# First keys and queries as float32 through SyncE and ScalarE, and units 2 to 7 in another order

## The chip, the cores and the metric

The kernel runs on one core of one Trainium2 chip. A core has five engines with instruction streams of their own: TensorE (PE in the profile; its weight loads are listed as PEld), VectorE (DVE), ScalarE (ACT), GpSimd (POOL) and SyncE (SP). Data moves between the main memory and the on-chip memory by DMA; an engine issues a DMA, and 16 DMA engines carry it out. The metric is the device time of one execution in microseconds; lower is better. Tests of the kernel before gave 285.56, 285.60 and 286.12 us, median 285.6.

## The reference

A sliding-window attention is followed by a two-layer network with a quick GELU. All inputs and the output are float32.

```python
B, H, S, D = 8, 8, 576, 64            # q, k, v: each 9.4 MB
scores = q @ k.T / sqrt(D)            # per batch and head
scores = where(|i - j| <= 32, scores, -1e9)
attn = softmax(scores)
x = (attn @ v) as [B * S, H * D]      # 4608 rows of 512
h = x @ w_in                          # w_in: 512 x 2048
out = (h * sigmoid(1.702 * h)) @ w_out   # w_out: 2048 x 512
```

## The kernel before

The 4608 rows are cut into 36 units of 128 queries (shifted by 32 rows against the keys, so that a window of 32 on both sides needs one unit of keys and 64 more) and into 9 tiles of 512 rows, four units each. For a unit, `scores` multiplies keys by queries and takes the exponential on ScalarE, `band` multiplies by a 0/1 mask on VectorE, `values` multiplies by v, with a column of ones that gives the sum, and `norm` divides on VectorE. `odd_v` copies v into a second arrangement, shifted by 64 rows, that every second block of queries needs: part 0 from the unit's own v, part 1 from the next unit's. `x_T` (one unit) and `x_T2` (two) transpose the result on TensorE for layer 1.

For a tile, layer 1 is either plain (`layer1_plain`: one step `d` of 256 columns of w_in, for one half of the tile's rows, eight matmuls and one GELU) or by seven products instead of eight (`l1_group`), which needs sums of weights (`w1_sums`, `w2_sums`) and of data (`x_sums`, `g_sums`) from VectorE. Tile 0 is computed plainly, tiles 1 to 8 by seven products. Layer 2 of a tile runs mixed into the next tile's layer 1: `self.do(self.l2, n)` takes the next n of its matmuls off a list.

The order of all this is written out by hand: each engine executes its instructions in the order of the program, and the framework adds only the waits for data and buffers. PSUM has banks with the tags A, B, C, E, LA, LB and t (two banks); a step that takes a tag waits until the one that had it before is read.

`opening` (L561) does the first units and tile 0. Its inputs come through POOL's DMA queue, which casts float32 to 16 bits on the way, in this order: first keys (320 rows) and first queries (256 rows) of batch 0, v of units 0 to 2, the first quarter of w_in, the second keys and second queries (256 rows each, up to the end of unit 3), the second quarter of w_in, v of units 3 and 4, the third quarter, keys and queries of units 4 to 7 (`load_four`), the fourth quarter, v of units 5 and 6, the first quarter of w_out, v of units 7 and 8, the rest of w_out, and then loads unit by unit (`fetch`). Between these issues POOL also builds the identity (`make_identity`) and the mask (`setup_mask`, `cut_mask`). A POOL issue waits, by the trace, until the load that stands eight places before it has landed.

`T_first` (L156) transposes the first or second keys or queries on TensorE; each half of the heads goes to one bank, and VectorE or ScalarE copies it out. Where TensorE has to wait at the start, `keep_busy` gives it junk matmuls on a zeroed tile. `first_layer1` (L845) is layer 1 of tile 1; its list `dv` holds VectorE's sums, taken off between the products.

## Time and profile before

| what | value |
| --- | --- |
| median of three runs | 285.6 us |
| the profiled execution's own time | 285.75 us |
| its span, first to last instruction | 284.0 us |
| granted TensorE clock | 1.000 |
| PE busy | 272.8 us, 96% |
| DVE busy | 217.2 us, 76% |
| ACT busy | 193.9 us, 68% |
| POOL busy | 126.9 us, 45% |
| PE busy from 0 to 24 us / 24 to 45 us / 45 to 284 us | 17.45 / 20.52 / 234.78 us |
| read from main memory / written to it | 36.83 MB / 9.44 MB |

A line of the timeline gives start, duration, engine, source line, operation, the tile written and the tile read, shapes, and in brackets how long the engine stood idle before it and what ended that. A line of the table of stages gives for a stretch of time its length, then the busy time (and number of instructions) of PE, PEld, DVE, ACT and POOL, the granted clock, the share of the DMA engines and the GB/s that they wrote. A line of the chain gives start, duration and whose work the end waited for. Times are from the start of the span. PE's time from 0 to 24 us holds junk as well as work, and its matmuls overlap, so that a busy PE need not be one at its peak.

### The profile page before, as it was taken

The page shows a single profiled execution, that of the slowest core. Times are in us where ns is not written, and L with a number is a line of the kernel's source. Part 1 is how long each engine was busy: PE and PEld are TensorE (multiplying, and loading weights), DVE is VectorE, ACT ScalarE, POOL GpSimd, SP SyncE. Part 2 cuts the span into 40 slices and gives each one's busy share as a digit, 9 for nine tenths or more (in the row PEclk, how much of TensorE's full clock was granted, in tenths as well). Part 3 has the DMA queues.
Part 4 walks back from the last instruction along what each step waited for, and adds up shares of the span by engine and source line. Part 5 has one row for each costly group of instructions (what it writes and reads, how often), then busy time and mean ns, then how long its engine had stood idle before and what let it go on. Part 6 is the DMA issues. An engine that isn't in the chain of part 4 may idle for free.

```text
span 284.0 us, 8953 instructions
## 1 busy us (share of the span) xinstructions
PE 272.8 (96%) x3684; PEld 223.3 (79%) x3684; DVE 217.2 (76%) x501; ACT 193.9 (68%) x340; POOL 126.9 (45%) x192
## 2 busy tenths in 40 slices
PE   6787999999999998999999999999999999999995
PEld 2466847776778887888888888888888888888884
DVE  1754997898887877798879887878788878946731
ACT  2556684799886778667966796689658875568411
POOL 8975446898599726739083909340110000000000
PEclk9999999999999999999999999999999999999999
DMA  8999999999999999999999999995422030201024
GB/s 90 182 193 196 184 204 159 193 124 147 136 154 152 200 127 195 124 203 143 201 102 189 131 203 82 198 146 140 132 58 71 26 113 14 81 2 74 2 95 133
DMA packets 149610, 37.63 MB, mean 132 GB/s; under 512 B 138048, under 2 KB 145216, under 8 KB 149568
## 3 DMA queue, kind: packets, MB, share of 16 engines
q0 software_dynamic: 106000, 18.42, 95.0%
q1 hardware_dynamic: 43120, 18.10, 34.2%
q8 instruction: 29, 0.48, 0.7%
q10 hardware_dynamic: 448, 0.52, 0.6%
q14 instruction: 13, 0.11, 0.1%
HBM read 36.83 MB, written 9.44 MB: 163 GB/s over the span
## 4 chain that ended last, share of the span: by engine, by line
PE 82%; DMA 7%; DVE 5%; POOL 4%; issue 1%; ACT 0%; DVEq 0%; POOLq 0%
PE o L70 37%; PE h L70 36%; PE pv L70 4%; DMA w<-in_moe_w_in_dram 4%; DMA xT<-x 3%; PE sc L70 3%; POOL ve L198 1%; POOL kq L142 1%; DVE xs L353 1%; DVE vo L209 1%; PE tp L321 1%; PE tp L231 1%; DVE a L334 1%; PE tp L188 1%; POOL w L115 1%
## 5 line engine op out<-in xcount | busy, mean ns | idle before, releaser
L418 ACT ACTIVATE g<-h 128x512 f16<-128x512 f32 x128 | 72.2, 598 | 35.7 <-PE h L70 34.9
L70 PEld LDWEIGHTS <-g 128*128 128x128 f16 x576 | 54.4, 98 | 9.5
L70 PEld LDWEIGHTS <-a 128*128 128x128 f16 x512 | 49.1, 97 | 12.3 <-DVE xs L353 2.2
L70 PE MATMUL h<-xs,a 128*128 128x256 f16 x384 | 57.6, 272 | 0.9 <-DVE xs L353 0.7
L70 PE MATMUL o<-w,g 128*128 128x256 f16 (+1 forms) x320 | 55.5, 294 | 0.0
L70 PEld LDWEIGHTS <-w 128*128 128x128 f16 x512 | 48.9, 98 | 8.4 <-DMA w<-in_moe_w_in_dram 1.7
L70 PE MATMUL h<-xT,w 128*128 128x256 f16 x384 | 54.0, 273 | 1.4 <-DMA w<-in_moe_w_in_dram 1.4
L209 POOL COPY vo<-ve 64x264 int32<-64x264 int32 x55 | 25.5, 463 | 61.3 <-PE pv L70 59.0
L70 PEld LDWEIGHTS <-gs 128*128 128x128 f16 x384 | 36.8, 98 | 4.7
L255 ACT ACTIVATE p<-sc 128x512 bf16<-128x512 f32 x72 | 36.9, 620 | 2.6 <-PE sc L70 2.5
L70 PE MATMUL o<-b,gs 128*128 128x256 f16 x256 | 37.6, 273 | 0.0
L70 PE MATMUL o<-b,g 128*128 128x256 f16 x256 | 37.5, 273 | 0.0
L198 POOL DMA_DIRECT2D ve<-in_v_dram x40 | 34.4, 865 | 6.2 <-DMA qst<-in_q_dram 2.8
L431 DVE TENSOR_TENSOR h<-h,s 128x512 f32<-128x512 f32 x32 | 22.3, 698 | 17.8 <-PE h L70 17.5
L131 POOL DMA_DIRECT2D qst<-in_q_dram x35 | 28.1, 804 | 3.5 <-DMA w<-in_moe_w_out_dram 2.8
L67 ACT COPY h<-h 128x512 f32<-128x512 f32 x32 | 18.9, 589 | 15.5 <-PE h L70 15.1
L293 DVE TENSOR_TENSOR x<-pv,rec 128x256 f16<-128x256 f32 (+1 forms) x53 | 27.6, 520 | 1.8
L131 POOL DMA_DIRECT2D kst<-in_k_dram x31 | 26.4, 855 | 5.0 <-DMA ve<-in_v_dram 2.6
L437 DVE TENSOR_TENSOR h<-h,s 128x512 f32<-128x512 f32 x32 | 22.4, 700 | 4.6 <-PE h L70 3.9
L263 DVE TENSOR_TENSOR p<-p,mask 128x1024 bf16<-128x1024 bf16 x36 | 25.0, 698 | 0.8 <-ACT p L255 0.6
L67 ACT COPY s<-h 128x512 f32<-128x512 f32 x32 | 19.2, 599 | 2.0 <-PE h L70 0.7
L70 PE MATMUL h<-xs,w 128*128 128x256 f16 x128 | 19.2, 273 | 0.0
(83 smaller groups left out, 343.7 us busy)
## 6 DMA issues: line engine op xcount, KB each, us to landing
out_dram<-o_sb SPq DMA_DIRECT2D x33, 256.0 KB, 4.6
ve<-in_v_dram POOLq DMA_DIRECT2D x32, 128.0 KB, 6.6
kst<-in_k_dram POOLq DMA_DIRECT2D x25, 128.0 KB, 6.6
qst<-in_q_dram POOLq DMA_DIRECT2D x21, 128.0 KB, 6.1
w<-in_moe_w_in_dram POOLq DMA_DIRECT2D x4, 512.0 KB, 8.9
w<-in_moe_w_out_dram POOLq DMA_DIRECT2D x4, 512.0 KB, 12.6
qst<-in_q_dram POOLq DMA_DIRECT2D x7, 96.0 KB, 6.4
kq<-in_q_dram POOLq DMA_DIRECT2D x2, 256.0 KB, 5.9
```

What stands on the lines that cost most here:

```text
L67: (eng.copy if eng is self.nc.scalar else eng.tensor_copy)(out, in_)
L70: self.nc.tensor.matmul(out, lhsT, rhs, start=start, stop=stop, skip_group_check=True)
L115: self.nc.gpsimd.dma_start(self.w1[:, :, c * 512:c * 512 + w], self.w_in[:, c * 512:c * 512 + w].rearrange("(k p) f -> p k f", p=128))
L131: self.nc.gpsimd.dma_start(t[off:off + n], src[b, :, s:s + n, :].rearrange("h s d -> s h d"))
L198: self.nc.gpsimd.dma_start(t[off:off + n, :, :self.D], self.v[b, :, s:s + n, :].rearrange("h s d -> s h d"))
L209: eng.tensor_copy(*((words(vo[64:128]), words(self.ve[u % 9][64:128])), (words(vo[0:64]), words(nxt)))[i])
L255: self.nc.scalar.activation(p[:, eo].rearrange("k h s -> k (h s)"), sc[eo], AF.Exp, scale=self.scale)
L263: (eng or self.nc.vector).tensor_mul(pv, pv, msk.to_broadcast([128, 8, 2, SQ]))
L293: dve.tensor_mul(x[:, 4 * at:4 * (at + n), :].rearrange("p (b h) d -> p b h d", b=n), acc[:, :, :, :D], r.to_broadcast([128, n, 4, D]))
L418: act.activation(g[:, f, 256 * half:256 * half + 256], bank.rearrange("p (i n) -> p i n", i=2), AF.Gelu_apprx_sigmoid)
L431: dve.tensor_add(e, b, s7)
L437: dve.tensor_add(c, b, s7)
```

## The change

The first keys and first queries no longer go through POOL with a cast. SP and ACT load them as float32, SP heads 0 to 3 into partitions 0 to 63 and ACT heads 4 to 7 into partitions 64 to 127, two DMAs each. New functions `cast` and `early` turn them into bfloat16 in the tile that also takes the second keys and queries: of the keys VectorE casts three of five row groups and ScalarE two, of the queries each two of four. The first queries lie four rows to a partition instead of two. `T_first` transposes them from both halves of the partitions in turn, and can leave one copy for later (`late_copy`).

The identity and the mask come from one `iota` on POOL and small VectorE operations, and the mask is cut by VectorE. `load_w1` takes a column instead of a quarter's number.

In the opening, there are fewer junk matmuls; the second keys are transposed between x_T of units 0 and 1, the second queries before layer 1's first step; the scores of units 2 and 3 stand before its second step; units 2 and 3 are transposed one by one, one copy on VectorE and one on ScalarE. The second quarter of w_out is loaded before v of units 7 and 8. The odd_v copies of units 6 and 7 move from ahead of the first band to between the norms; one step of layer 1 moves between values(6) and values(7); and w1_sums((3,), 1) moves from the opening to the head of `dv` in `first_layer1`. Later on, x_T2(10) becomes x_T of units 10 and 11.

```diff
@@ -97,23 +97,27 @@
         self.spark = cst.tile([128, 1], F32, name="spark")
     def setup_mask(self):
...
+        D = self.work.tile([128, 128], F32, name="gap", tag="s7", bufs=2)
+        self.nc.gpsimd.iota(D, pattern=[[-1, 128]], base=0, channel_multiplier=1,
+                            allow_small_or_imprecise_dtypes=True)
+        dve = self.nc.vector
+        dve.tensor_single_scalar(self.ident, D, 0.0, op=ALU.is_equal)
+        dve.tensor_copy(self.identh, self.ident)
+        for r in (slice(0, 64), slice(64, 128)):
+            d = D[r, r].rearrange("p (b s) -> p b s", b=1).to_broadcast([64, 2, SQ])
+            up = int(r.start > 0)
+            for blk, op in ((2 * up, ALU.is_ge), (2 - 2 * up, ALU.is_le)):
+                dve.tensor_single_scalar(self.mask[r, blk:blk + 2, :], d, 0.0, op=op)
     def cut_mask(self):
         lo, hi = slice(0, 64), slice(64, 128)
         for b, rows, cols in ((0, hi, slice(0, 32)), (0, lo, slice(32, 64)), (2, lo, slice(0, 32)), (2, hi, slice(32, 64))):
-            self.nc.gpsimd.memset(self.mask[rows, b, cols], 0.0)
-    def load_w1(self, c, n=1):
-        w = 512 * n
-        self.nc.gpsimd.dma_start(self.w1[:, :, c * 512:c * 512 + w],
-                                 self.w_in[:, c * 512:c * 512 + w].rearrange("(k p) f -> p k f", p=128))
+            self.nc.vector.memset(self.mask[rows, b, cols], 0.0)
+    def load_w1(self, lo, n=512):
+        self.nc.gpsimd.dma_start(self.w1[:, :, lo:lo + n],
+                                 self.w_in[:, lo:lo + n].rearrange("(k p) f -> p k f", p=128))
     def load_w2(self, c):
         self.nc.gpsimd.dma_start(self.w2[:, 4 * c:4 * c + 4, :],
@@ -132,15 +136,34 @@
-    FIRST = {"k": ((0, 320, 5, 0), (320, 256, 2, 5)), "q": ((32, 256, 2, 7), (288, 256, 2, 9))}
+    FIRST = {"k": ((0, 320, 5, 0), (320, 256, 2, 5)), "q": ((32, 256, 4, 0), (288, 256, 2, 7))}
     def load_first(self, c, part):
-        if "first" not in self.stage:
-            self.stage["first"] = self.sb("g", [128, self.H, 11, self.D], BF16, 2, "kq1")
         lo, n, j, at = self.FIRST[c][part]
-        src = {"q": self.q, "k": self.k}[c]
-        self.nc.gpsimd.dma_start(self.stage["first"][0:n // j, :, at:at + j],
-                                 src[0, :, lo:lo + n, :].rearrange("h (p j) d -> p h j d", j=j))
+        src = {"q": self.q, "k": self.k}[c][0, :, lo:lo + n, :].rearrange("h (p j) d -> p h j d", j=j)
+        if part:
+            if "first" not in self.stage:
+                self.stage["first"] = self.sb("g", [128, self.H, 9, self.D], BF16, 2, "kq1")
+            self.nc.gpsimd.dma_start(self.stage["first"][0:n // j, :, at:at + j], src)
+            return
+        s = self.stage["early", c] = self.sb(*{"k": ("g", [128, 4, j, self.D], F32, 2),
+                                               "q": ("xs", [128, 4, j, self.D], F32, 1)}[c], "early")
+        for i in range(2):
+            (self.nc.sync, self.nc.scalar)[i].dma_start(s[64 * i:64 * i + 64], src[:, 4 * i:4 * i + 4])
+    def cast(self, c, engs):
+        at = 0
+        for eng, m in engs:
+            self.copy(eng, self.early(c)[:, :, at:at + m], self.stage["early", c][:, :, at:at + m])
+            at += m
+    def early(self, c):
+        j = self.FIRST[c][0][2]
+        h = 4 * (c == "q")
+        return self.stage["first"][:, h:h + 4, 0:j]
     def kq_tile(self, t):
@@ -158,16 +181,27 @@
         lo, n, j, at = self.FIRST[c][part]
         lo -= 32 * (c == "q")
         dst = self.kq_tile(0)["kq".index(c)][:, :, lo:lo + n]
-        r = slice(0, n // j)
-        src = self.stage["first"][r]
-        for i, (tag, eng) in enumerate(zip(tags, engs)):
-            tp = self.bank(tag, [128, 2, j, n // j], BF16, "tp")
-            for h in range(4):
-                for x in range(j):
-                    self.nc.tensor.transpose(tp[64 * (h % 2):64 * (h % 2) + 64, h // 2, x, :],
-                                             src[:, 4 * i + h, at + x, :], self.ident[r, r])
-            self.copy(eng, dst[:, 2 * i:2 * i + 2, :].rearrange("x h (p j) -> x h p j", j=j),
-                      tp.rearrange("x h j p -> x h p j"))
+        m = n // j
+        tps = [self.bank(tag, [128, 2, j, m], BF16, "tp") for tag in tags]
+        def one(i, h, x):
+            if part:
+                r, src = slice(0, m), self.stage["first"][0:m, 4 * i + h, at + x, :]
+            else:
+                r = slice(64 * i, 64 * i + 64)
+                src = self.early(c)[r, h, x, :]
+            self.nc.tensor.transpose(tps[i][64 * (h % 2):64 * (h % 2) + 64, h // 2, x, :], src, self.ident[r, r])
+        both = [(i, h, x) for i in range(2) for h in range(4) for x in range(j)]
+        for y in both if part else sorted(both, key=lambda y: y[::-1]):
+            one(*y)
+        for i, eng in enumerate(engs):
+            ap = (dst[:, 2 * i:2 * i + 2, :].rearrange("x h (p j) -> x h p j", j=j),
+                  tps[i].rearrange("x h j p -> x h p j"))
+            if eng is None:
+                self.late_copy = lambda e, ap=ap: self.copy(e, *ap)
+            else:
+                self.copy(eng, *ap)
     def load_four(self, c):
@@ -568,35 +602,36 @@
             dve.memset(t[:, :, self.D:], 1.0)
         self.load_first("k", 0)
         self.load_first("q", 0)
-        make_identity(nc, self.ident)
+        self.setup_mask()
+        self.cut_mask()
         act.activation(self.spark, self.spark, AF.Exp)
...
         self.load_w1(0)
-        self.setup_mask()
         self.load_first("k", 1)
         self.load_first("q", 1)
-        self.cut_mask()
-        self.load_w1(1)
+        self.load_w1(512)
         self.load_v(3)
         self.load_v(4, slice(0, 1))
-        self.load_w1(2)
+        self.load_w1(1024)
         self.load_v(4, slice(1, 2))
         self.load_four("k")
         self.load_four("q")
-        self.load_w1(3)
-        dve.tensor_copy(self.identh, self.ident)
-        self.keep_busy(10, "E", 512)
+        self.load_w1(1536)
+        self.keep_busy(8, "E", 512)
+        self.cast("k", ((dve, 3), (act, 2)))
+        self.cast("q", ((dve, 2), (act, 2)))
         self.T_first("k", 0, "AC", (dve, act))
-        self.keep_busy(2, "E", 512)
+        self.keep_busy(1, "E", 512)
         self.T_first("q", 0, ("LA", "LB"), (dve, act))
...
         self.load_w2(0)
+        self.load_w2(1)
         for u in (7, 8):
             self.load_v(u)
-        for c in (1, 2, 3):
+        for c in (2, 3):
             self.load_w2(c)
         self.load_kq("k", 8)
         self.scores(0, "t")
@@ -610,11 +645,12 @@
         self.norm(0)
         self.values(1, "AC")
         self.norm(1)
-        self.keep_busy(2, "E", 512)
-        self.x_T(0, "LA", act)
         self.keep_busy(1, "E", 512)
-        self.x_T(1, "LB", act)
-        self.T_first("k", 1, "AC", (dve, dve))
+        self.x_T(0, "t", act)
+        self.T_first("k", 1, ("LA", "LB"), (None, dve))
+        self.x_T(1, "B", act)
+        self.late_copy(act)
+        self.T_first("q", 1, "EC", (dve, act))
         h, n, gelus = [], [0], []
         def l1(half, *ds):
@@ -622,26 +658,26 @@
                 self.layer1_plain(0, d, half, h[n[0] % len(h)])
                 n[0] += 1
-        self.layer1_plain(0, 0, 0, "B", gelus)
-        self.T_first("q", 1, ("LA", "LB"), (dve, act))
-        self.layer1_plain(0, 1, 0, "E", gelus)
-        self.odd_v(2, dve)
-        self.odd_v(3, dve, (0,))
-        h[:] = ["B", "E", "LA", "LB"]
+        self.layer1_plain(0, 0, 0, "A", gelus)
         self.scores(2, "t")
-        self.scores(3, "AC")
+        self.scores(3, "BE")
+        self.layer1_plain(0, 1, 0, "C", gelus)
+        self.odd_v(2, dve, (0,))
+        self.band(2)
+        self.odd_v(2, dve, (1,))
+        self.odd_v(3, dve)
         self.layer1_plain(0, 2, 0, "LA", gelus)
+        self.values(2, "t")
+        self.band(3)
+        self.norm(2)
         self.layer1_plain(0, 3, 0, "LB", gelus)
+        self.values(3, "BE")
         self.do(gelus)
-        self.band(2)
-        self.odd_v(3, dve, (1,))
-        self.band(3)
-        self.values(2, "t")
-        self.norm(2)
-        self.values(3, "AC")
         self.norm(3)
+        h[:] = ["A", "C", "LA", "LB", "B", "E"]
         l1(0, 4)
-        self.x_T2(2, "A", dve)
+        self.x_T(2, "t", dve)
+        self.x_T(3, "B", act)
         l1(0, 5)
         dve.tensor_copy(self.k_first, self.kT[0][:, :, 0:64])
         dve.tensor_copy(self.v_first, self.ve[0][0:64])
@@ -653,6 +689,7 @@
         dve.tensor_copy(self.kT[4][:, :, 0:64], halo)
         l1(1, 2, 3)
         self.T_four("q", "AC", (dve, act))
+        h[:], n[0] = ["LA", "LB"], 0
         l1(1, 4, 5)
         self.odd_v(4, dve)
         self.scores(4, "t")
@@ -660,8 +697,7 @@
         self.odd_v(5, dve)
         for i in (3, 1, 2, 4):
             self.w1_sums((i,), 0)
-        self.odd_v(6, dve)
-        self.odd_v(7, dve, (0,))
+        self.odd_v(6, dve, (0,))
         for d, tag in ((6, "B"), (7, "E")):
             self.layer1_plain(0, d, 0, tag, gelus)
         self.do(self.l2, 3)
@@ -672,27 +708,27 @@
         self.do(self.l2, 2)
         self.band(4)
         self.band(5)
-        self.odd_v(7, dve, (1,))
         self.band(6)
         self.values(4, "t")
         self.norm(4)
+        self.odd_v(6, dve, (1,))
         self.band(7)
+        self.odd_v(7, dve, (0,))
         self.values(5, "AC")
         self.norm(5)
+        self.odd_v(7, dve, (1,))
         self.do(self.l2, 8)
         self.values(6, "t")
         self.norm(6)
-        self.do(self.l2, 2)
+        h[:], n[0] = "BE", 0
+        l1(1, 6)
         self.values(7, "AC")
         self.norm(7)
-        h[:] = "BE"
-        n[0] = 0
-        self.w1_sums((3,), 1)
-        l1(1, 6, 7)
+        l1(1, 7)
         self.x_T2(4, "A", act)
         self.do(self.l2, 2)
         self.x_T2(6, "t", dve)
-        self.do(self.l2, 4)
+        self.do(self.l2, 6)
     def fetch(self, u):
         self.load_kq("q", u)
@@ -826,7 +862,8 @@
         self.norm(11)
         self.scores(14, "BE")
         do(more, 8)
-        self.x_T2(10, "C", dve)
+        self.x_T(10, "A", dve)
+        self.x_T(11, "C", act)
         self.scores(15, "t")
         do(self.x_sums(2))
         self.seed2 = dve
@@ -844,7 +881,7 @@
     def first_layer1(self):
-        dv = [lambda i=i: self.w1_sums((i,), 1) for i in (1, 2, 4)]
+        dv = [lambda i=i: self.w1_sums((i,), 1) for i in (3, 1, 2, 4)]
         for n in range(4):
             if n == 3:
                 self.turn(12)
```

7 lines of the change are left out of this document (removed).

## The prediction

> **What bounds the kernel now.** I read the page's slices first: TensorE (PE) is full from the third slice to the last, so the end moves only by what the opening gains or what PE work grows. Here is PE and what the DMA engines wrote:
>
> ```profile
> PE   6787999999999998999999999999999999999995
> GB/s 90 182 193 196 184 204 159 193 124 147 136 154 152 200 127 195 124 203 143 201 102 189 131 203 82 198 146 140 132 58 71 26 113 14 81 2 74 2 95 133
> ```
>
> Then a table of stages. Up to 24 us PE is busy 17.45 us, some of it junk matmuls; in 24 to 45 us it lacks 0.48 us:
>
> ```profile
> 0.00:24.00 24.00, 17.45 (x314) 10.64 (x314) 12.93 (x41) 12.00 (x20) 18.50 (x35) 1.00 1.42 159
> 24.00:45.00 21.00, 20.52 (x346) 15.11 (x344) 16.84 (x36) 14.03 (x22) 10.34 (x13) 1.00 1.55 192
> ```
>
> In single microseconds the last column (GB/s written) climbs slowly, then stays between 154 and 217 with no gap; the loads shrink float32 to 16 bits, so twice that is read. Around 38 us PE (third number) is short:
>
> ```profile
> 2.00:3.00 1.00, 1.00 (x4) 0.35 (x3) 0.00 (x0) 0.30 (x2) 1.00 (x2) 1.00 0.21 9
> 3.00:4.00 1.00, 1.00 (x4) 0.41 (x3) 0.20 (x1) 0.00 (x0) 0.93 (x4) 1.00 0.76 68
> 4.00:5.00 1.00, 1.00 (x5) 0.21 (x2) 0.00 (x0) 0.00 (x0) 1.00 (x2) 1.00 1.32 191
> 7.00:8.00 1.00, 0.99 (x18) 0.48 (x16) 0.53 (x2) 0.61 (x1) 0.88 (x3) 1.00 2.42 154
> 16.00:17.00 1.00, 1.00 (x22) 0.69 (x20) 0.74 (x2) 0.01 (x1) 0.75 (x2) 1.00 1.24 208
> 38.00:39.00 1.00, 0.70 (x15) 0.19 (x8) 0.97 (x3) 1.00 (x3) 0.62 (x1) 1.00 1.24 198
> 39.00:40.00 1.00, 0.84 (x33) 0.69 (x34) 1.00 (x3) 0.98 (x2) 0.12 (x1) 1.00 1.24 207
> ```
>
> The chain of the opening runs over POOL's issues, then one load (w1 columns 1024 to 1535), then PE:
>
> ```profile
> 13.27 10.13 DMA w<-in_moe_w_in_dram
> 23.40 0.05 issue
> 23.44 1.05 PE h L70 x8
> ```
>
> The timeline shows every earlier step starting as its load lands: transposes of the second keys at 14.75, of the second queries at 16.30, layer 1 on w1's second quarter at 18.75. So the opening follows the DMA stream, and that stream is full from 4 us on. What matters is when it starts. From 35.6 us it is so again with w2: layer 2's first matmuls (35.75) and its next eight (39.90) start as POOL is let go by a landed w2 quarter (35.66, 39.88).
>
> **The change, part by part.** *First keys and queries.* POOL loses two issues (0.82 and 0.90 us); SP and ACT each get two. POOL starts the first one at 1.33, and bytes come slowly: 77 KB by 4.0 us, which at 191 GB/s is 0.4 us of full flow, so the stream is as if it had begun at 3.6. SP and ACT are free at 0.82 (ACT's first instruction; SP's wait is the same 0.8). What SP needs from issue to flow is shown by the last stores:
>
> ```profile
> 275.09 5.63 SPq L459 DMA_DIRECT2D out_dram<-o_sb  x3
> ```
>
> and by the bytes written in each quarter of a microsecond behind that issue:
>
> ```profile
> 275.50:275.75 0.25, 0.25 (x5) 0.23 (x3) 0.00 (x0) 0.14 (x1) 0.00 (x0) 1.00 0.00 0
> 275.75:276.00 0.25, 0.25 (x5) 0.23 (x3) 0.00 (x0) 0.24 (x1) 0.00 (x0) 1.00 0.20 70
> 276.00:276.25 0.25, 0.25 (x5) 0.22 (x4) 0.00 (x0) 0.00 (x0) 0.00 (x0) 1.00 1.04 352
> ```
>
> Issue at 275.09, as if begun at 275.95: 0.86 us. So the new stream begins at 0.82 + 0.86 = 1.7, 1.9 earlier. If the slow climb (first bytes about 2.75, full from 3.6: 0.85) belongs to the first reads and not to POOL, it begins at 0.82 + 0.66 + 0.85 = 2.35, 1.25 earlier. A store isn't a load; I take 1.6 and keep 1.25 and 1.9. The bytes read are the same. That they are also written as float32 costs nothing if reading limits; see the rival below.
>
> *The path of units 0 and 1.* k reads 0.655 MB, q 0.524 MB; at 2 x 191 GB/s that is 1.7 and 1.4 us. From 2.0 on, with the 0.7 us that lay between k's bytes (3.6 + 1.7 = 5.3) and its transposes (6.01), k lands at 4.4 and q at 5.8, up to 6.5 where v's packets mix in; I take 6.1. The casts are new. ACT's 512 elements: 0.58 (its 128x512 copies). DVE's 768 and 512: no row; 0.69 for 128x512 float32 from PSUM above, 0.217 for a 128x256 bf16 copy (so 0.43) below; I take 0.58. q: 6.1 + 0.58, 32 transposes at 0.87/40 us each (0.7), copy 0.69: scores at 8.1 against 8.64. At the bad end (q 6.5, cast 0.69, transposes 0.7 beneath k's copy of 0.82 on DVE, then q's 0.69: 8.7) they start when they do now, or 0.5 later if DVE's casts take twice that. Behind DVE's wait for q are the copies of transposed k and so both units' scores. Units 0 and 1 then end x_T(1)'s transposes near 14.2 now and 13.7 after; the second queries land 16.3 - 1.6 = 14.7. So even a start 0.5 later is covered, and this path costs and gives nothing.
>
> *Mask, identity, cut.* POOL loses some 2.8 us (0.22 + 0.29 + 0.36 + 4 x 0.29 + 4 x 0.14) and gets one iota, about 0.29 like the 128x128 select. DVE gets six small operations of 0.2 (the 128x128 cast is 0.195) and four memsets of about 0.1, 1.6 us, between iota's end near 1.9 and k's landing at 4.4; 0.5 or so would spill into the casts if each took twice that. POOL then reaches the second keys' issue near 5.0 instead of 8.67: 3.6 earlier, more than the stream's 1.6, so issuing doesn't hold it. Later issues wait for the load eight before, as now (w1's last waits 1.56 for its second), and so move with the stream.
>
> Does DVE's work hold POOL's issues? Three v issues take 2.66 us with DVE's 0.195 us cast among them, 0.89 each, the median of all: not visible. I take nothing; the other end is a rival below.
>
> *Units 2 and 3.* The order changes (k1 before x_T(1), scores before the second layer-1 step, split x_T with half the copies on ACT), with about the same operations. From the second queries to scores is 1.55 us (16.30 to 17.85), to the last norm's end 7.3 (23.63). From 14.7 that ends at 22.0, beside w1's third quarter at 21.8. No gain or loss besides the stream's; x_T's copy on ACT, 0.58, waits behind four gelus but lies beside a layer-1 step of 0.9.
>
> *Junk* falls from 20 to 15 matmuls, all beneath waits. The first ones take 0.42 us each until 4.24, then 0.22; eight last till 4.65, still past that point. If not, transposes run at half speed for about 1 us, in the covered path.
>
> *Units 4 to 7.* odd_v of units 6 and 7 (1.28 us plus a 0.35 us wait for v7) leaves its place before the first band; w2's second quarter goes ahead of v7 and v8, arriving 0.52 MB or 1.3 us earlier. Now PE lacks 0.30 + 0.16 in 38 to 40 us, waiting for bands. That goes: at most -0.5, since PE lacks 0.48 in all there. Against it w1_sums(3, 1), 0.68, moves into first_layer1, where DVE is busy 9.2 of 10 us (50 to 60): up to +0.7. v7 then comes 2.6 us later relative to the stream (1.05 MB), 36.5 - 1.6 + 2.6 = 37.5, and its copy now stands after norm(4), near 38: not late. I take -0.4. The late x_T2(10) becomes two transposes and copies: 0 (bounds +-0.2, one more instruction in a full PE).
>
> **Sum.** -1.6 - 0.4 = -2.0 on the profiled execution's own 285.75 (span 284.0 and 1.75 around it): 283.75. It stands 0.15 over the median of 285.6, so 283.6. Its own range, from 285.6: 1.9 + 0.5 + 0.2 off gives 283.0; 1.25 off and 0.2 on, with nothing from units 4 to 7, gives 284.55.
>
> **Rivals.** *Only issue time is saved.* The Trainium skill (DMA: Bandwidth & Descriptors, Issuing engines are not separate DMA queues) says DMAs of all issuers share the same engines, and more issuers save only the time to initiate. As a mechanism here: flow is limited after the issue, and the start moves only 1.33 - 0.82 = 0.5. For it: the slow climb may be the reads'. Against: 1.42 us from POOL's issue to bytes, 0.66 from SP's. Time: 285.6 - 0.5 - 0.4 = 284.7. Chance 0.11.
>
> *The DVE bill.* DVE holds POOL for as long as its new work lasts, 1.6 us of mask and some 0.9 us of casts beside POOL's issues; POOL's lead over the stream is 3.6 - 1.6 = 2.0, so 0.5 comes through, and w1_sums adds its 0.7: 285.6 - 1.6 - 0.4 + 1.2 = 284.8; chance 0.08. Against the first half stands the 0.89 us above, against the second nothing but the 0.8 us that DVE has free in 50 to 60. The Trainium skill (SBUF — State Buffer, SBUF: two separate sides) has the first half as a rule: a float32 copy from SBUF to SBUF on DVE locks GpSimd out, which then can't write descriptors. The trace of before has no such copy, so it neither shows nor denies it.
>
> *Slower: writing float32 limits.* No load of now writes over 217 GB/s. If that is a limit of loads, k and q (1.18 MB) take 5.7 us at 207 instead of 3.1, the whole stream is 2.6 - 1.6 = 1.0 later, and the time is 285.6 + 1.0 - 0.4 = 286.2. It decides from 1.18 MB / (3.1 + 2.0) us = 231 GB/s downward. Against it: float32 stores run at 352 above. Chance 0.09.
>
> **Chances and range.** The forecast 0.68; better than its range (PE also fills part of its idle before 24 us) 0.04; the rivals 0.28 as given. Measurement tells apart about 0.2%, 0.57 us: faster is under 285.03. Faster: forecast, better and 0.09 of the two middle rivals' 0.19, 0.81. Within 0.2%: 0.07 of those two, where the gain of units 4 to 7 fails too. Slower: the float32 rival and their last 0.03, 0.12. Range 282.6 to 285.6, leaving out the slower cases and a little below.
>
> **What would show it.** Right: GB/s over 150 by 2 to 3 us, near 380 written while k and q arrive; transposes at about 5; second queries' transposes near 14.7; layer 1 on w1's third quarter at 21.8 instead of 23.44; PE full in 38 to 40; everything after the same with an offset of 2. Wrong: written rate near 200 in the first microseconds; the casts starting after 6; POOL's issues stretched over 1 us while DVE casts; scores of unit 2 later than 17; PE gaps for DVE sums in 47 to 62.

## The result and the profile after

The changed kernel is slower: 287.26 us, median of five runs (286.62 to 287.86), against 285.60 for before on the same chip (five runs, 285.35 to 286.12). The ratio is 1.0054, with a 95% interval of 1.0032 to 1.0076. The forecast was 283.6, with a range up to 285.6. The profiled execution took 287.26 us, its span 285.5, so it is 1.5 us longer than the one of before both ways.

The page's slices of the changed kernel show where it went. A digit is the busy share of a slice of 7.1 us in tenths, for PEclk the granted clock. TensorE is at 50% in the first two slices, where it had 60 and 70%, and its granted clock falls in the second:

```profile
PE   5599999999999998999999999999999999999995
...
PEclk9689999999999999999999999999999999999999
...
GB/s 151 179 193 195 194 194 163 195 136 147 138 136 137 190 131 200 152 178 137 202 118 184 129 183 122 210 119 149 125 58 69 33 110 15 79 2 76 1 106 119
```

The table of stages of the changed kernel (length, then busy time of PE, PEld, DVE, ACT and POOL, granted clock, DMA share, GB/s written):

```profile
2.00:3.00 1.00, 1.00 (x4) 0.43 (x3) 0.88 (x6) 0.85 (x1) 1.00 (x2) 1.00 0.54 114
3.00:4.00 1.00, 1.00 (x4) 0.33 (x3) 0.13 (x3) 0.63 (x2) 1.00 (x2) 1.00 0.99 309
4.00:5.00 1.00, 0.79 (x2) 0.00 (x0) 0.00 (x0) 0.00 (x0) 1.00 (x3) 1.00 1.12 231
5.00:6.00 1.00, 0.00 (x0) 0.00 (x0) 0.00 (x0) 0.00 (x0) 1.00 (x2) 1.00 1.19 226
...
9.00:10.00 1.00, 0.00 (x0) 0.00 (x0) 0.07 (x1) 0.09 (x1) 0.00 (x0) 0.50 3.68 135
38.00:39.00 1.00, 1.00 (x28) 0.49 (x27) 1.00 (x2) 1.00 (x3) 0.00 (x0) 1.00 2.10 154
39.00:40.00 1.00, 1.00 (x26) 0.57 (x25) 1.00 (x3) 1.00 (x3) 0.87 (x1) 1.00 1.75 190
...
0.00:24.00 24.00, 17.05 (x318) 10.36 (x319) 13.62 (x47) 12.10 (x21) 14.67 (x22) 0.86 1.48 176
```

The bytes do come earlier (114 GB/s between 2 and 3 us, where before had 9), but the rate falls to 231 and 226 while keys and queries are still on their way. These bytes are float32, read and written alike. In the first 10 us the kernel wrote 154 GB/s x 10 us = 1.54 MB, of which 1.18 MB are float32, so it read 1.18 + 2 x 0.36 = 1.90 MB. Before wrote 1.12 MB in the same time (112 GB/s, all 16 bits), so it read 2.24 MB. The new stream starts earlier and at 10 us is 0.34 MB behind; at before's 0.38 MB per us that is 0.9 us. Runs 8 and 15 below have the instructions of before up to 42 us, 3 and 16 those of the changed kernel; in these 10 us they wrote the same within 1 GB/s.

TensorE's timeline of the changed kernel shows what waited for it (start, duration, line, output, count, in brackets the idle time before and what ended it):

```profile
7.10 0.51 PE L193 MATMUL tp<-ident,kq 64*64 64x64 bf16 x40 [2.31 <-DVE kq L67]
10.41 0.64 PE L193 MATMUL tp<-ident,kq 64*64 64x64 bf16 x32 [2.48 <-DVE kq L67]
11.93 1.07 PE L70 MATMUL sc<-kq 64*64 64x64 bf16 x48 [0.34 <-DVE kq L67]
...
16.47 0.40 PE L343 MATMUL tp<-identh,x 128*128 128x128 f16 x4
...
17.78 0.64 PE L193 MATMUL tp<-ident,kq 128*64 128x128 bf16 x16
...
24.35 1.05 PE L70 MATMUL h<-xT,w 128*128 128x256 f16 x8 [0.36 <-DMA w<-in_moe_w_in_dram]
```

In the chain of waits the last of these steps still follows the landing of w_in's third quarter, as in before:

```profile
10.94 13.36 DMA w<-in_moe_w_in_dram
24.35 1.05 PE h L70 x8
```

That is 24.35 against 23.44: in this pair of executions the opening lost 0.9 us where 1.6 was to be gained. The landing varies more than the bytes do: in runs 3 and 16 this step starts at 23.98 and 23.95, in runs 8 and 15 at 22.51 and 22.66. So the loss at this step is between 0.5 and 1.8 us, and 0.9 is the value of one pair.

Later there is one more place. TensorE of the changed kernel, in the timeline, stands still at 73.6 us for a sum of VectorE; between 71 and 76 us before shows no idle time of TensorE. First the changed kernel's lines, then VectorE's line of before that makes the same sum:

```profile
73.15 0.69 DVE L297 TENSOR_TENSOR p<-p,mask 128x1024 bf16<-128x1024 bf16 x1 [0.29 <-ACT p L289]
73.76 0.42 DVE L400 TENSOR_TENSOR g<-g 128x512 f16<-128x512 f16 x1
...
74.24 0.39 PE L70 MATMUL o<-b,g 128*128 128x256 f16 x2 [0.63 <-DVE g L400]
```

```profile
69.74 0.51 DVE L366 TENSOR_TENSOR g<-g 128x512 f16<-128x512 f16 x1
...
72.66 0.69 DVE L263 TENSOR_TENSOR p<-p,mask 128x1024 bf16<-128x1024 bf16 x1 [0.22 <-ACT p L255]
```

In before that sum is made at 69.74, ahead of two `band` products; in the changed kernel it comes behind them, 4 us later, though the kernel as a whole is only 0.5 late there.

### The profile page after: what moved, and what is told of

Same layout as the page of the kernel before. It is cut to its first block, busy times and chain, and to the rows that moved or that the text cites. A ratio compares the mean times of both kernels' runs of the same rounds, so it can differ in the third digit from the quotient of the medians.

```text
span 285.5 us, 8986 instructions
## 1 busy us (share of the span) xinstructions
PE 272.7 (96%) x3694; PEld 223.7 (78%) x3695; DVE 218.8 (77%) x511; ACT 196.5 (69%) x345; POOL 122.9 (43%) x180
## 4 chain that ended last, share of the span: by engine, by line
PE 81%; DMA 11%; ACT 4%; DVE 2%; issue 1%; POOL 0%; POOLq 0%; DVEq 0%; ACTq 0%
PE h L70 37%; PE o L70 36%; DMA w<-in_moe_w_in_dram 5%; PE pv L70 4%; DMA ve<-in_v_dram 3%; DMA xT<-x 3%; PE sc L70 2%; ACT p L289 2%; DVE xs L387 1%; ACT L289 1%; PE tp L222 1%; PE tp L265 1%; ACT g L452 1%; PE tp L355 0%; PE tp L343 0%
## 5 line engine op out<-in xcount | busy, mean ns | idle before, releaser
L243 POOL COPY vo<-ve 64x264 int32<-64x264 int32 x55 | 24.8, 451 | 61.1 <-PE pv L70 58.6
```

Source lines behind the costliest of these rows:

```text
L243: eng.tensor_copy(*((words(vo[64:128]), words(self.ve[u % 9][64:128])), (words(vo[0:64]), words(nxt)))[i])
```

## The experiments

**How they are compared.** VectorE adds `h` and `s` twice in each `l1_group`; the first of the two comes 32 times in the program. The start of the same addition in two traces gives how late one kernel is against the other at that point. The table has this lateness against the profiled execution of before (minus: ahead), at the additions that before makes at 66, 84, 101, 112 and 263 us, and the ratio of the times to before's on the same chip. Single executions there differ more than on the first chip (before: 284.9 to 290.6 us, medians 285.9 to 286.4), so verdicts are read from ratios. A trace is one execution: at 66 us before, 8 and 15 lie up to 0.68 us apart and 5 and 6 1.25 us, though each group has the same instructions up to about 40 us. The profiled execution of 1 is the fastest of its twelve (285.27, median 286.48), those of 3, 5 and 6 are over 1 us slower than their medians. So a lateness of some tenths tells little by itself; a step between two points tells more where many traces repeat it.

| kernel | ratio, 95% interval | 66 | 84 | 101 | 112 | 263 |
| --- | --- | --- | --- | --- | --- | --- |
| the changed kernel | 1.0054 (1.0032 to 1.0076) | +0.49 | +1.13 | +1.13 | +1.15 | +1.16 |
| 1: first loads by POOL again | 0.9997 (0.9977 to 1.0016) | -0.89 | -0.26 | -0.25 | -0.66 | -0.56 |
| 2: before, with the float32 loads only | 1.0063 (1.0032 to 1.0094) | +2.30 | +2.31 | +2.31 | +1.84 | +2.12 |
| 3: w1_sums and x_T2 back | 1.0018 (0.9991 to 1.0044) | +0.18 | +0.19 | +0.19 | +2.28 | +3.38 |
| 4: loads over all partitions | 0.9971 (0.9948 to 0.9994) | -1.34 | -0.70 | -0.70 | -1.47 | -1.43 |
| 5: as 4, with more junk | 0.9977 (0.9949 to 1.0005) | -1.60 | -0.96 | -0.95 | +0.07 | +0.09 |
| 6: as 5, w1_sums and x_T2 back | 0.9997 (0.9973 to 1.0021) | -0.35 | -0.34 | -0.34 | +0.27 | +0.26 |
| 7: changed kernel, more junk | 1.0056 (1.0027 to 1.0085) | +0.16 | +0.93 | +0.93 | +1.02 | +1.60 |
| 8: before, with w1_sums moved | 1.0009 (0.9990 to 1.0028) | +0.68 | +1.33 | +1.33 | +1.57 | +1.59 |
| 9: as 4, but halves of the partitions | 1.0084 (1.0060 to 1.0109) | +2.02 | +2.50 | +2.69 | +3.51 | +3.49 |
| 10: before, with the loads of 4 | 0.9997 (0.9973 to 1.0022) | -0.48 | -0.46 | -0.46 | +0.53 | +0.52 |
| 11: as 6, junk at two more places | 0.9981 (0.9955 to 1.0007) | -1.60 | -1.59 | -1.59 | -0.65 | -0.66 |
| 12: as 11, x of two units on TensorE | 1.0008 (0.9998 to 1.0018) | -1.59 | -1.59 | -0.48 | -0.35 | -0.37 |
| 13: as 12, at other places | 1.0093 (1.0060 to 1.0126) | -1.41 | -1.40 | -0.32 | +1.49 | +1.51 |
| 14: as 12, by x_T2 in bank B | 0.9945 (0.9928 to 0.9963) | -1.46 | -1.46 | -1.46 | -1.58 | -1.58 |
| 15: before, with that x_T2 | 0.9991 (0.9965 to 1.0017) | +0.09 | +0.11 | +0.11 | -0.55 | -0.57 |
| 16: changed kernel, with that x_T2 | 1.0034 (1.0016 to 1.0052) | +0.36 | +0.83 | +1.02 | +0.36 | +0.70 |

### Is it the loads? (1 and 2)

Undo the loads alone in the changed kernel, and put them alone into before:

```diff
-        for i in range(2):
-            (self.nc.sync, self.nc.scalar)[i].dma_start(s[64 * i:64 * i + 64], src[:, 4 * i:4 * i + 4])
+        self.nc.gpsimd.dma_start(self.stage["first"][0:n // j, :, at:at + j], src)
...
-        self.cast("k", ((dve, 3), (act, 2)))
-        self.cast("q", ((dve, 2), (act, 2)))
```

> The changed kernel, but the first keys and queries go through POOL with the cast again, 128 partitions for the queries as before the change; mask on VectorE, order of units 2 to 7 and w1_sums as changed. Theory A (the float32 loads through SP and ACT arrive late: queries at 9.9 us, v at 9.9 to 10.5, and hold the whole opening back): the queries' transposes start near 7.4 us, layer 1 on w1's third quarter at 23.4 or earlier, the shift against the kernel before at 49 us (a VectorE addition of tile 1's layer 1) is 0 or below instead of +0.49, the loss of 0.6 between 66 and 84 us stays; 285.5 to 286.2. Rival D (the new order of units 2 to 7 loses the time): shift at 49 us stays near +0.5; 287 or more.

> The kernel before with only the float32 loads through SP and ACT, the casts and the transposes from both halves of the partitions; mask on POOL and the old order. Theory A: the queries are cast near 10 us, w1's third quarter is used 0.9 us or more later than 23.44, nothing of it is paid back by the order, nothing is lost between 66 and 84; shift at 49 us +0.9 to +1.5, 286.5 to 287.1. Rival D: 285.6 or faster.

Without the float32 loads the changed kernel goes from a ratio of 1.0054 to 0.9997, and its interval ends below the other's start; with them alone before goes to 1.0063, and the interval lies above 1. So the loads lose the time. In the traces the first is 0.9 us ahead at 66 us and the second 2.3 late (+0.9 to +1.5 was expected), so the rest of the change gains in the opening: the same loads are 2.30 us late in the old order and 0.49 in the new. The step of +0.63 between 66 and 84 us stays in the first and is absent in the second: it is not from the loads.

### The list of sums (3 and 8)

```diff
-        dv = [lambda i=i: self.w1_sums((i,), 1) for i in (3, 1, 2, 4)]
+        dv = [lambda i=i: self.w1_sums((i,), 1) for i in (1, 2, 4)]
...
-        self.x_T(10, "A", dve)
-        self.x_T(11, "C", act)
+        self.x_T2(10, "C", dve)
```

with `self.w1_sums((3,), 1)` in the opening again. The other kernel is before with only `w1_sums((3,), 1)` moved to the head of `dv`.

> The changed kernel with w1_sums((3,), 1) back in the opening after norm(7), and x_T2(10) in place of x_T(10) and x_T(11). Theory B (VectorE falls one operation behind in first_layer1, its sub on g is pushed behind the bands, TensorE waits 0.63 for it at 74 us; x_T(11) on ScalarE costs 0.1): the shift at 84 us is that of 49 us, +0.5, and the time is 0.6 lower, 286.6. Rival (the step between 66 and 84 comes from the late start, not from these two edits): the shift still grows by 0.6, 287.2.

> The kernel before with one edit: w1_sums((3,), 1) moved from the opening to the head of first_layer1's list. Theory B: nothing or a slight gain at 49 us, a step of +0.5 to +0.65 between 66 and 84 us, TensorE waiting about 0.6 for VectorE's sub on g near 73; ratio 1.0015 to 1.0025. Rival (the extra operation fits VectorE's free 0.8 us): no step, ratio 1.000 or below.

The step is gone in the one (0.18 to 0.19) and there in the other (0.68 to 1.33), of the same size. In the whole table it is 0.47 to 0.77 in the eight traces with this move and at most 0.02 in the nine without it. The timeline of before with w1_sums moved has the line of the changed kernel again:

```profile
74.42 0.39 PE L70 MATMUL o<-b,g 128*128 128x256 f16 x2 [0.63 <-DVE g L366]
```

So this single move costs 0.65 us in the trace, at 74 us and not where it was put (50 us). The ratio of 8, 1.0009, is below the 1.0015 to 1.0025 that were expected, and its interval holds both 0 and 0.65 us. x_T(10) and x_T(11) in place of x_T2(10) cost nothing: 0.64 with them, 0.65 without.

That the kernel with the move begins 0.68 late at 66 us does not come from it, for its instructions up to 42 us are those of before. TensorE's timeline shows w_in's third quarter used at 22.51, 0.93 us earlier than in the trace of before; then layer 2's eight matmuls wait for a quarter of w_out until 40.30, where before starts them at 39.90 without a wait:

```profile
22.51 1.05 PE L70 MATMUL h<-xT,w 128*128 128x256 f16 x8 [0.40 <-DMA w<-in_moe_w_in_dram]
...
40.30 1.89 PE L70 MATMUL o<-w,g 128*128 128x512 f16 x8 [1.26 <-DMA w<-in_moe_w_out_dram]
```

So in this opening a lead at 23 us need not reach 49 us. In the other kernel the profiled execution lost 2.1 us between 101 and 112, of which below.

### Float32, or 64 partitions? (4 and 9)

Two readings of the 226 GB/s: float32 is slow to write, or a load into 64 partitions is. The first of two kernels spreads every load over all 128 partitions (keys as 384 rows of three to a partition, queries two to a partition; SP heads 0 to 3, ACT heads 4 to 7), the second has the same rows, the same 768 and 512 bytes in a piece, but half of the partitions per load, with all heads:

```diff
-            (self.nc.sync, self.nc.scalar)[i].dma_start(s[64 * i:64 * i + 64], src[:, 4 * i:4 * i + 4])
+            (self.nc.sync, self.nc.scalar)[i].dma_start(s[:, 4 * i:4 * i + 4], src[:, 4 * i:4 * i + 4])
```

```diff
-            (self.nc.sync, self.nc.scalar)[i].dma_start(s[:, 4 * i:4 * i + 4], src[:, 4 * i:4 * i + 4])
+            (self.nc.sync, self.nc.scalar)[i].dma_start(s[64 * i:64 * i + 64], src[64 * i:64 * i + 64])
```

> The changed kernel, but each of the four float32 loads covers all 128 partitions (keys 384 rows as 128 x 3, second keys 192 rows; queries 256 rows as 128 x 2; SP heads 0 to 3, ACT heads 4 to 7); same bytes in all. Theory P (a load into 64 partitions is written at only 0.2 MB per us, and the loads follow one another): written rate 0.35 MB per us or more from 3 us, queries cast by 6, v landed by 8, about 285.3. Rival Q (the queues of SP, ACT and POOL take turns or share badly whatever the partitions): queries cast at 9 to 10, about 287.2.

> e4_all_partitions with one edit: each load brings all eight heads into 64 partitions (SP the lower, ACT the upper half) instead of four heads into 128. The same runs of 768 and 512 bytes, the same bytes, the same transposes. Theory P (64 partitions to a load limit the written rate to 0.2 MB per us and the queues follow one another): 200 to 250 GB/s in 4 to 8 us, queries' transposes near 10 us, shift at 49 us +0.2 or more. Rival R (e4 was faster by the shorter runs or the other transposes): 350 GB/s, as e4.

The tables of stages, first with all partitions, then with halves:

```profile
3.00:4.00 1.00, 1.00 (x4) 0.33 (x3) 0.13 (x3) 0.36 (x2) 1.00 (x2) 1.00 1.08 362
4.00:5.00 1.00, 0.79 (x2) 0.00 (x0) 0.00 (x0) 0.00 (x0) 1.00 (x3) 1.00 1.11 358
5.00:6.00 1.00, 0.00 (x0) 0.00 (x0) 0.55 (x1) 0.55 (x1) 1.00 (x2) 1.00 1.20 297
```

```profile
3.00:4.00 1.00, 1.00 (x4) 0.33 (x3) 0.13 (x3) 0.66 (x2) 1.00 (x2) 1.00 0.83 247
4.00:5.00 1.00, 0.79 (x2) 0.00 (x0) 0.00 (x0) 0.00 (x0) 1.00 (x3) 1.00 1.12 241
5.00:6.00 1.00, 0.00 (x0) 0.00 (x0) 0.00 (x0) 0.00 (x0) 1.00 (x2) 1.00 1.12 222
```

From 4 to 5 us float32 is written at 358 GB/s over all partitions and at 241 in halves, with the same pieces; the changed kernel, halves with pieces of 1280 and 1024 bytes, writes 231. So here the number of partitions of a load decides, and the sizes of the pieces do not. The times say the same: the two kernels differ by this one edit, at 0.9971 and 1.0084. The DMA queues of the microsecond from 4 to 5 us (packets, MB, share of 16 engines; q1 is SP's queue, q10 ACT's) show how, in the changed kernel and with all partitions:

```profile
q1 hardware_dynamic: 165, 0.20, 97.4%
q10 hardware_dynamic: 28, 0.03, 14.2%
```

```profile
q10 hardware_dynamic: 275, 0.20, 59.1%
q1 hardware_dynamic: 307, 0.16, 52.4%
```

With halves one load at a time gets about 0.2 MB per us and the other nearly stands, though they write different partitions (in the next microsecond ACT's queue has 91% and SP's 16, 0.19 and 0.03 MB); with all partitions both run together. The Trainium skill (SBUF — State Buffer, Can I just issue two DMAs to hit both halves?) says that loads into partitions 0 to 63 and 64 to 127 do not add up, and its Door 1 section gives about 218 GB/s for 64 partitions; from 4 us on the 0.20 MB per us here agree, and the 362 of loads over 128 are beyond it. Before 4 us they do not agree: from 3.5 to 4 us only ACT's queue moves in the kernel with halves, into 64 partitions, and it writes 349 GB/s:

```profile
3.50:4.00 0.50, 0.50 (x3) 0.15 (x1) 0.00 (x0) 0.17 (x1) 0.50 (x1) 1.00 1.02 349
```

So 64 partitions are no fixed limit in these traces; why the rate falls after 4 us, they do not show. Over the whole of 2 to 6 us the three kernels with halves (the changed one, 2 and 9) write 192 to 220 GB/s, 4 and 10 with all partitions 298 and 291.

### Junk (5, 7 and, with both mendings, 6 and 11)

```diff
-        self.keep_busy(8, "E", 512)
+        self.keep_busy(12, "E", 512)
```

in the kernel with all partitions; 18 and 12 junk matmuls in the changed kernel; 12 with w1_sums and x_T2 put back; and then six behind the first odd_v and two ahead of x_T(0).

> e4_all_partitions with only the 12 junk matmuls. Theory J: keys' transposes at 22 ns each, scores of units 0 and 1 0.7 us earlier (9.1 instead of 9.8); whether the end gains is open: where the first layer-1 step on w1's third quarter waits for its load (22.0), nothing; where for units 2 and 3, up to 0.7. Step of +0.65 between 66 and 84 stays.

> The changed kernel with 18 junk matmuls ahead of the keys' transposes and 12 between these and the queries', so that TensorE has no idle stretch from 8 to 10 us. Theory A (the clock's fall to 0.50 from 9 to 15.6 us is a consequence and costs little, since w1's third quarter lands at 24.3 all the same): clock 1.00 throughout, scores at 11.6 instead of 11.9, shift at 49 us still +0.3 to +0.5, time 286.9 to 287.3. Rival C (the half clock is the loss of the opening): shift at 49 us 0 or below, 286.6 or less.

> e4_all_partitions with w1_sums((3,), 1) and x_T2(10) back where they were before the change, and 12 junk matmuls instead of 8 ahead of the casts. Theories P, B and J (eight junk matmuls end before TensorE reaches its fast spacing, so that the first transposes and scores run at half speed: 62 ns a transpose in e4 against 22 before) together: transposes of the keys at about 22 ns each, the shift against before at 49 us -1.4 to -2.2, the same shift at 84 us (no step of +0.65), 0.994 to 0.995 of the time before. If the step of 66 to 84 us comes from an early start, it stays at +0.65.

> e5_late_and_junk with six junk matmuls instead of four after odd_v of units 0 and 1, and two instead of one ahead of x_T(0), so that TensorE's clock doesn't fall to 0.50 from 15 to 18.6 us as in e5's execution. Theories P, B and J: clock 1.00, shift at 49 us -1.4 to -1.7, the same at 84 us, ratio 0.994 to 0.996. What remains uncertain is the stage at 105 to 110 us, where TensorE waits for a DMA transpose between 0 and 2 us from execution to execution.

With eight junk matmuls the first transposes run slowly (24 in 1.50 us; with twelve in 0.87), though the granted clock stands at 1.00. That makes the scores only 0.3 us earlier (9.76 to 9.48), since they then wait for copies, and the time is the same. In the changed kernel the clock stays at 1.00 with more junk, and it gains 0.3 us at 66 us and no time. So the half clock from 9 to 15.6 us is a consequence of the late loads and worth at most 0.3 us there.

The last two also have w1_sums and x_T2 back, and should have led by 1.4 us or more at 49 and at 84 us. No step is left in them, but 6 leads by only 0.35 us at 66 us, where 5 leads by 1.60. In this execution of 6 the granted clock is 0.50 from 16 to 18 us, in that of 5 it is 1.00; in 11, with junk at two more places, it is 1.00 too, and the lead 1.60. So a half clock there goes with a loss of 1.25 us; no run parts the clock from what else differs between the executions. And of the leads of 0.34 and 1.59 at 101 us, 0.6 and 0.94 were lost by 112 us.

### The old order with the good loads (10)

```diff
+            (self.nc.sync, self.nc.scalar)[i].dma_start(s[:, 4 * i:4 * i + 4], src[:, 4 * i:4 * i + 4])
...
-        self.keep_busy(10, "E", 512)
+        self.keep_busy(12, "E", 512)
+        self.cast("k", ((dve, 2), (act, 1)))
+        self.cast("q", ((dve, 1), (act, 1)))
```

> The kernel before with only the float32 loads of e4_all_partitions (128 partitions each), the casts, and 12 junk matmuls; mask on POOL, old order, w1_sums in its old place. This is the first term of the prediction alone with loads at full rate: second queries' transposes at 14.7 to 15.6 instead of 16.3, shift at 49 us -0.7 to -1.6, no step between 66 and 84, ratio 0.995 to 0.998. If the gain of e4 came from the order of units 2 to 7, the shift is near 0.

The stream is fast (329 and 361 GB/s), yet only 0.48 us come of it. The casts put the first scores at 9.83 instead of 8.64, and the second queries, which stand behind layer 1's first step, are transposed at 17.02 instead of 16.30 (14.7 to 15.6 was expected). So the stream brings less than the first term of the prediction even at full rate. That the new order is needed to use it is not shown: at 66 us the loads alone lead by 0.48 (10), the rest of the change without them by 0.89 (1), both together by 1.34 (4) and 1.60 (5), which is about the sum. In the times each alone is at 0.9997, and both together at 0.9971 and 0.9977.

### Where the lead goes between 101 and 112 us (12 to 16)

In before VectorE waits there for DMA transposes of x (tile 3, issued by SP at 98.9 us), and TensorE for VectorE. The timelines of before and of the kernel with both mendings (11):

```profile
109.61 0.42 DVE L353 TENSOR_TENSOR xs<-xT 128x512 f16<-128x512 f16 x1 [1.45 <-DMA xT<-x]
...
110.09 0.61 PE L70 MATMUL h<-xs,a 128*128 128x256 f16 x4 [0.69 <-DVE xs L353]
```

```profile
106.52 0.44 PE L70 MATMUL sc<-qT,kT 64*64 64x64 bf16 x22 [1.03 <-DMA kT<-kst]
...
108.96 0.43 DVE L378 TENSOR_TENSOR xs<-xT 128x512 f16<-128x512 f16 x1 [2.48 <-DMA xT<-x]
```

The kernel is 1.6 us earlier, the transposes land only 0.65 earlier. It is not so in every execution: in that of 4 the same sum starts at 108.14, and its lead grows from 0.70 to 1.47 in this stage. The edit takes the transposes away from the DMA engines:

```diff
-                    self.x_T(u + n)
+                    if n == 1:
+                        self.x_T(u + n)
...
         do(late, 2)
-        do(l2, 20)
+        do(l2, 4)
+        if t == 3:
+            self.x_T2(u - 2, "B", self.nc.vector)
+        do(l2, 16)
```

This is the third form (14). The two ahead of it took the bank t: unit 14 ahead of values(15) and unit 15 behind the last group; then unit 14 behind values(15) and unit 15 behind the scores.

> The kernel of all-partition loads, w1_sums((3,), 1) back in the opening, x_T2(10) back and more junk (ratio 0.9981; its profiled execution was 1.59 us ahead of before at 101 us and 0.65 at 112), with one more edit: x of units 14 and 15 of tile 3 is transposed on TensorE, with a copy on ScalarE, instead of by DMA transposes. Theory G: that lead is lost because the DMA transposes issued at 98 to 101 us land at 108 to 109.6 us whatever the opening did. Then VectorE's x_sums of tile 3 wait no more for a transpose, the lead at 112 us is 1.2 to 1.5 us (TensorE pays about 0.2 for eight transposes), and the ratio is 0.994 to 0.997. Rival: another load ends that stage too (the transposed keys, which TensorE's scores waited for by 1.03 us); then x_sums wait no more, but the lead at 112 us is still 0.5 to 0.8, and the ratio 0.997 to 0.999.

> As the run before, but each of the two transposes of x on TensorE (units 14 and 15) stands where a bank with the tag t is free: unit 14 behind values(15) with its copy on ScalarE, unit 15 behind the scores of units 16 and 17 with its copy on VectorE. In the run before TensorE waited 0.83 and 0.94 us for the copies out of that bank, and that hid what theory G speaks of. Theory G (x's DMA transposes alone end the stage of 101 to 112 us): the lead of 1.59 us at 94 us is 1.2 to 1.5 at 112 us, no wait over 0.4 us is left between, ratio 0.994 to 0.997. Rival (the transposed keys kT, which TensorE waited for by 1.03 us at 106.5, end it as well): TensorE waits 0.7 us or more for kT, the lead at 112 us is 0.4 to 0.9, ratio 0.997 to 1.000.

> As the two runs before, but x of units 14 and 15 is transposed together by one x_T2 into the bank B, between layer 2's matmuls behind the scores of units 16 and 17, where that bank is free; the bank with the tag t, which the two runs before made TensorE wait for (0.83 and 0.94 us, 1.03 and 2.45 us), is left alone. One copy of 1024 elements on VectorE, some 0.8 us, comes ahead of its sums. Theory G (x's DMA transposes alone end the stage of 101 to 112 us): TensorE pays 0.45 us (0.22 from one group of four transposes to the next matmul in the run before), nothing waits over 0.4 us more, the lead of 1.6 us at 94 is 1.1 to 1.7 at 112 us (before waits 0.69 there itself), ratio 0.994 to 0.997. Rival (the transposed keys end it as well): TensorE waits 0.7 us or more for kT at 106 us, the lead at 112 is 0.3 to 0.9, ratio 0.997 to 1.000.

The first two put waits for that bank in place of the other (0.83 and 0.94 us at 98.78 and 104.25 in the one, 1.03 and 2.45 us at 99.33 and 106.52 in the other, by TensorE's timeline) and settled nothing. In the third the transposes cost TensorE 0.45 us (103.11 to 103.56), VectorE's sum starts at 106.97 with no wait, and for the keys 0.34 are left:

```profile
103.11 0.61 PE L346 MATMUL tp<-identh,x 128*128 128x128 f16 x8
...
106.20 0.44 PE L70 MATMUL sc<-qT,kT 64*64 64x64 bf16 x22 [0.34 <-DMA kT<-kst]
...
106.97 0.42 DVE L378 TENSOR_TENSOR xs<-xT 128x512 f16<-128x512 f16 x1
```

The whole lead comes through (1.46 at 101, 1.58 at 112 and to the end), and the time is 0.9945 of before, 284.63 us against 286.14: faster than both kernels. The executions of 11 take 284.20 to 287.43 us, those of 14 take 284.18 to 285.50: the best are alike, and with the edit the late ones are missing. Then the same edit in before and in the changed kernel:

> The kernel before with the one edit of the last run (x of units 14 and 15 by x_T2 into bank B instead of by DMA transposes), nothing of the change. If the edit alone carried the last run (0.9945), this one gives 0.994 to 0.996 too. If the opening's lead carries it and the edit only lets it through (theory G), this one gains what before waited at 110 us less TensorE's 0.45 us: 0.69 - 0.45 = 0.24 us in a profiled execution, ratio 0.997 to 1.000.

> The changed kernel with the same one edit. The change's own losses (opening, w1_sums, x_T's copy; +1.15 us at 84 us and later) should then stand alone, without the stage of 101 to 112 us: 1.1 to 1.2 us more than the run with before and this edit, at every point from 84 us on; ratio to before 1.001 to 1.005. If the edit mends something of the change that I have not seen, the distance between these two is under 0.7 us.

Alone it is worth nothing that can be measured (0.9991), and the opening without it is at 0.9981. So the opening makes the gain and the edit lets it through. The changed kernel stays slower with it, by 1.27 us against before with it (287.29 and 286.02); its losses are its own. In the two traces it is 0.27 us behind at 66 us, 0.72 at 84, 0.91 at 112 and 1.27 at 263, where 1.1 to 1.2 was expected from 84 us on.

## Why the prediction was wrong

**The start of the stream: the issue right, the size wrong.** SP and ACT issue at 0.74 us (forecast 0.82). The stages of a quarter of a microsecond, first of the changed kernel, then of before:

```profile
2.00:2.25 0.25, 0.25 (x2) 0.15 (x1) 0.25 (x1) 0.10 (x1) 0.25 (x1) 1.00 0.03 10
2.25:2.50 0.25, 0.25 (x2) 0.05 (x1) 0.24 (x2) 0.25 (x1) 0.25 (x2) 1.00 0.88 179
```

```profile
2.75:3.00 0.25, 0.25 (x2) 0.04 (x1) 0.00 (x0) 0.00 (x0) 0.25 (x1) 1.00 0.82 36
```

The first bytes come near 2.25, 1.5 us after the issue, where the row of a store had given 0.66, and 0.5 us earlier than before's, which is the gain that the rival "only issue time is saved" had. By 4 us the changed kernel has read 0.42 MB and before 2 x 0.08; at 0.38 MB per us it is 0.7 us ahead, and not 1.6. With all partitions (4) it is 0.56 MB, 1.1 us ahead, so even there the term was too large. The rival still missed the time, since it has nothing for what comes next.

**"That they are also written as float32 costs nothing if reading limits": the step that failed.** The stream was to write near 380 GB/s and wrote 231 and 226 from 4 to 6 us. So 0.7 us ahead at 4 us became 0.9 behind at 10. Its term was -1.6 and came to +0.9 in bytes, and in this pair of traces also at w_in's third quarter. The slower rival had the place, the decision point (231 GB/s and less) and nearly the size (+1.0), at a chance of 0.09, but not the cause: float32 runs at 362 over all partitions. The edit that lost the time is "half of the heads on each half of the partitions", which the prediction costed at nothing and gave no word. The store that was held against the rival, at 352 GB/s, has all 128 partitions.

**Landing of k and q: wrong by the same cause.** k's casts start at 6.37 (k forecast for 4.4), q's at 9.93 (forecast 6.1), scores at 11.93 (forecast 8.1). The bound for a bad end was 0.5 late; it was 3.3. So the path of units 0 and 1 was no longer covered: TensorE is idle from 8 to 10 us, and the second queries' transposes come at 17.78 (forecast 14.7). v, which mixes in, lands 8.3 us after its issue, where before needs 4.8.

**The costs of the new operations: right.** The casts take 0.65 and 0.43 on VectorE and 0.62 on ScalarE (forecast 0.58); POOL's issues of v take 0.93 us each beside VectorE's mask, where 0.89 was the row of before. In run 1, with the same mask on VectorE, they take 0.89. So nothing shows that VectorE holds POOL, the first half of the DVE bill. The terms for POOL's mask add up to 2.6 us, not 2.8; nothing hangs on it, for the second keys are issued at 4.87 (forecast 5.0).

**Units 4 to 7: the place right, the size open.** TensorE is full from 38 to 40 us, and the lateness falls from 0.91 at w_in's third quarter to 0.49 at 49 us, 0.4 as forecast. But that this is the forecast's size is partly luck: between the same two points the executions of runs 8 and 15 lose 1.6 and 0.9 us against that of before, with its instructions.

**w1_sums: the size right, the place in the sum wrong.** "Up to +0.7" went into a rival; the sum had nothing. It costs 0.65, and the step is in every trace that has the move. The prediction looked at VectorE's 0.8 us free between 50 and 60 us; the bill came at 74, since the list of sums that runs later moves on by one entry past two `band` products.

**x_T2(10): right,** at 0. **Junk: wrong, and without effect:** eight were not past the point; the slow transposes cost 0.3 us of a covered path.

**"Everything after the same with an offset of 2": wrong, though the changed kernel hides it.** A lead of 1.6 shrinks to 0.65 between 101 and 112 us, since the DMA transposes of x land only 0.65 us earlier than in before; why they land when they do, the runs do not show. Before's trace had the wait (1.45 us) in view.

In this pair of traces the pieces add up: at 263 us the changed kernel is 1.16 late, 0.9 of the stream, -0.4 of units 4 to 7, 0.65 of w1_sums; the last store's landing adds 0.34, to 1.5 us. The first two of these are not sure to tenths. At 49 us three executions with the changed opening are 0.18, 0.35 and 0.49 us late, three with before's are 0, 0.09 and 0.68, so at that point the traces alone do not show a loss; that the loads in halves cost time is shown by the ratios, 1.0084 against 0.9971 (9 and 4) and 1.0063 against 0.9997 (2 and 10; 10 also has two more junk matmuls). How much of the 1.66 us between the medians each piece has stays open.

With the loads over all partitions, w1_sums where before has it and x_T2 in bank B, the same idea gives 1.58 us, where 2.0 was forecast. That these are near each other is luck in part: at 66 us the loads alone led by 0.48 us, not 1.6 (run 10), and the rest of the change by 0.89, not 0.4 (run 1).

## What to carry to other kernels

Before a load is split among queues, see how many partitions each part covers: two halves of the partitions from two queues gave 241 GB/s here, the same bytes with every load over all partitions 358. A move of work on an engine that runs a list in order is paid where that list next meets its consumer, which may be 20 us later; add it to the sum, not to a rival. A lead won in the opening reaches the end only if no later stage waits for transfers, so search the trace of before for DMA waits behind the opening too. And before a difference of two traces is split into tenths, see how far two executions of the same instructions lie apart: here up to 0.9 us at one step.

## What was unexpected of the hardware

With two loads of 64 partitions on SP's and ACT's queues, they take turns: one has 97% of the DMA engines' time in one microsecond, the other 91% in the next. v's packets, issued by POOL at 1.34 us, move their first bytes only at 5.5 us in the changed kernel (and after 6 us with all partitions), and by 6 us the two other queues have written 0.87 of their 1.18 MB (1.2 of 1.31); why POOL's queue stands behind, the runs do not show. DMA transposes issued at 98 to 102 us land 8 to 9 us later. And with eight junk matmuls transposes took 62 ns each instead of 36 at a granted clock that is shown as 1.00.
